# Attention rows and gate logits taken straight from the attention weights times [V, V's logits], in a fused attention and mixture-of-experts kernel

## Chip, cores and metric

One core of one Trainium2 chip runs the kernel. The metric is the device time of one execution in microseconds; a comparison takes the median of several executions. Engines are called by the names of the profile: PE (TensorE, its matrix instructions), PEld (TensorE's weight loads), DVE (VectorE), ACT (ScalarE), POOL (GpSimd), SP (SyncE, which here only issues DMAs).

## The reference, cut to what matters

Three parts follow each other. The change lies in the first; the other two are most of the time.

```python
# attention: 8 batches, 8 heads, 576 positions, 64 wide; K and V are averaged over groups of 8 positions
k_p = k.reshape(B, H, 72, 8, D).mean(axis=3)
v_p = v.reshape(B, H, 72, 8, D).mean(axis=3)
scores = np.matmul(q, k_p.transpose(0, 1, 3, 2)) / np.sqrt(D)
attn = np.exp(scores - scores.max(-1, keepdims=True))
attn = attn / (attn.sum(-1, keepdims=True) + 1e-09)
x = np.matmul(attn, v_p)                     # -> x: 4608 tokens x 512
# mixture of experts: 8 experts, 512 -> 1024 -> 512, the best two for each token
noisy = x @ w_gate + np.log1p(np.exp(x @ w_noise)) * noise
top2, weights = best_two(noisy)              # softmax over the two
x = sum(weights * (np.maximum(x @ w1[e], 0) @ w2[e]) for the two e)
# last layer: 512 -> 2048 -> 512
h = x @ w_in
out = (h - np.tanh(h)) @ w_out
```

## The kernel before, in words

The attention part is one loop over 36 tiles of 128 tokens (`NT` = 36). A tile holds 128 tokens of all 8 heads; four of the 36 tiles lie across the end of a batch and have rows of two batches ("mixed" tiles). A batch is four tiles, or five, counted from its first one: the first tiles of the eight batches, called T0, are 0, 4, 9, 13, 18, 22, 27 and 31. The loop is software-pipelined by hand: iteration t works on several tiles, each at another step. Every engine executes its own instructions in the order in which the program wrote them, so a wait of one instruction holds up all that stand behind it on that engine.

An iteration t of the loop does, in this order:

- `st_exps(t)`: ACT, eight exponentials, one per head, with sums.
- `st_xT(t-4)`: ACT copies the transposed x of an earlier tile from PSUM.
- first halves of the steps listed in `pe_step` for this t (PE: `vt`, `vs`, `kb`).
- `st_norm(t-1)` and `st_g(t-6)`: DVE. `st_norm` makes the reciprocals of the sums (`sm`, `rc`), `st_g` scales the rows of a finished tile (`xr`), scales its logits (`lg`) and adds them over the heads (`lz`); `xr` goes to DRAM by a DMA of SP.
- `st_attT(t-2)`: PE, five transposes of the weights into two PSUM tiles, and two ACT copies out of them.
- `st_q(t+2)`: PE transposes of q, and an ACT copy.
- `st_scores(t+1)`: PE; DVE takes two row maxima (`mx`), one for each half of the heads.
- `st_x(t-5)`: PE multiplies the transposed x by `wgn`, which is [identity, gate weights, noise weights]: it turns x back into rows and makes the logits beside them, in the tile `px`.
- second halves of the `pe_step` jobs, and then the jobs listed in `at_step` for this t (DVE and POOL work on K and V of coming batches, and weights of the next part).
- `st_av(t-3)`: PE, V times transposed weights, which gives x transposed.

Between them `tick` writes a few rows of the gate's work at a time (`gate_jobs`: top two, positions, lists of tokens per expert), for the tiles already finished, mostly on DVE.

Per batch, K and V (a `kt` or `vt` tile of 2560 elements per partition for each) are reduced over the 8 positions in three additions of 1280, 640 and 320 elements. The first was POOL's, the others DVE's. For K a `ke` product and the `kb` transposes follow; for V a maximum `vm`, its transpose (`vt`), its power of two (`vs`), and the product `vb` with a per-row scale `of8`, which writes `VB`.

PSUM has four buffers of the tag `pt` (transposes, small products, transposed x), two of `psc` (scores) and one of `px`. The instruction that first writes a buffer waits until the last reader of its former content is done.

The loop runs 42 iterations (36 and 6 more, in which the pipeline empties). The gate's last group of tiles and the gathering of the first rows for the experts happen in those last ones; then the experts' matmuls start (the line that writes `ph` from `x0T` and `pair`).

Of the kernel before, what the change touches and what calls it, by code (L numbers as in the profile page):

```python
# [10 lines left out]
F32 = mybir.dt.float32  # L11
# [4 lines left out]
OP = mybir.AluOpType  # L16
# [921 lines left out]
def attention(nc, tc, st, V):  # L938
# [52 lines left out]
    def warm(n, tag="px"):  # L991

        if tag == "px":
            p = ps.tile([128, HP, 256], F32, name="px", bufs=1)[:, 0:2].rearrange("p a c -> p (a c)")
        else:
            p = ps.tile([128, 4 * SP], F32, name=tag, bufs=2)
        for _ in range(n):
            nc.tensor.matmul(p, calm[:, 0:128], calm[:, 0:p.shape[1]], start=True, stop=True)
# [24 lines left out]
    ts(before, rowi, 0.0, None, op0=OP.is_gt)  # L1023
    ones = ep.tile([128, 128], BF16, name="ones")
    nc.vector.memset(ones, 1.0)
    wgn = one.tile([128, HP, 128 + 4 * E], F32, name="wgn")
    nc.vector.memset(wgn[:, :, 128:], 0.0)
    nc.vector.tensor_copy(wgn[:, :, 0:128], identf[:, None, :].to_broadcast([128, HP, 128]))
    nc.vector.memset(idx, 0)
    slot = ep.tile([128, 128], F16, name="slot")  # L1030
    nc.gpsimd.iota(slot, pattern=[[1, 128]], base=0, channel_multiplier=0, allow_small_or_imprecise_dtypes=True)
# [6 lines left out]
    for i in range(2):
        for w, o in ((w_gate, 0), (w_noise, E)):
            o += 128 + 2 * E * i  # L1040
            nc.sync.dma_start(wgn[64 * i:64 * i + 64, :, o:o + E], w.rearrange("(m i p) e -> i p m e", i=2, p=64)[i])
# [12 lines left out]
    def prep_jobs(b, first=False):  # L1054
        tl = {}

        def kpool():
            add(nc.vector, b, "k", 2)
            add(nc.vector, b, "k", 1)
            tl["ke"] = wk.tile([128, 5, 2, D], F32, name="ke", bufs=1)  # L1060
            tt(tl["ke"], KV[b, "k"][:, :, 0:1].to_broadcast([128, 5, 2, D]), odd[:, :, :, None].to_broadcast([128, 5, 2, D]),
               op=OP.mult)

        def vpool():
            add(nc.vector, b, "v", 2)
            add(nc.vector, b, "v", 1)
            tl["va"] = KV[b, "v"]

        def vmax():
            tl["vm"] = wk.tile([128, 1], F32, name="vm")  # L1070
            nc.vector.tensor_reduce(tl["vm"], tl["va"][:, :, 0], axis=AX.XY, op=OP.max, apply_absolute_value=True)

        def vmaxT():
            p = ps.tile([1, 128], F32, name="pt", bufs=4)
            nc.tensor.transpose(p, tl["vm"], identf)
            yield
            tl["vx"] = wk.tile([1, 1], F32, name="vx")
            nc.vector.tensor_reduce(tl["vx"], p, axis=AX.X, op=OP.max)

        def vscale():  # L1080
            p = ps.tile([128, 1], F32, name="pt", bufs=4)
            nc.tensor.matmul(p, ones1, tl["vx"], start=True, stop=True)
            yield
            m = wk.tile([128, 3], F32, name="vs")
            pow2(nc, m, p)
            of8 = wk.tile([128, 5, 4], F32, name="of8")
            ts(of8, of, m[:, 2:3], None, op0=OP.mult)
            tt(VB[b % 2].rearrange("p c (j d) -> p c j d", d=D), tl["va"][:, :, 0:1].to_broadcast([128, 5, 4, D]),
               of8[:, :, :, None].to_broadcast([128, 5, 4, D]), op=OP.mult)
            lo, hi = b * S, b * S + S  # L1090
            t0, t1 = lo // 128, -(-hi // 128)
            for t in range(t0, t1):
                o0, o1 = max(lo - 128 * t, 0), min(hi - 128 * t, 128)
                if o1 - o0 < 128:
                    ts(isc[o0:o1, t:t + 1], m[o0:o1, 1:2], 1.0 / 128, None, op0=OP.mult)
            f0, f1 = -(-lo // 128), hi // 128
            ts(isc[:, f0:f1], m[:, 1:2].to_broadcast([128, f1 - f0]), 1.0 / 128, None, op0=OP.mult)

        def kbd():
            for i, (c0, c1) in enumerate(((0, 3), (3, 5))):  # L1100
                w = cuts[c1] - cuts[c1 - 1]
                p = ps.tile([128, 4, 128], F32, name="pt", bufs=4)[:, 0:c1 - c0, 0:w]
                for c in range(c0, c1):
                    nc.tensor.transpose(p[:, c - c0], tl["ke"][:w, c].rearrange("p i d -> p (i d)"), identf[:w, :w])
                o = KB[b % 2][:, cuts[c0]:cuts[c1]].rearrange("p (c n) -> p c n", n=w)
                nc.scalar.activation(o, p, AF.Copy, scale=1.0 / 512)
            yield
        return dict(k=kpool, v=vpool, vm=vmax, vt=vmaxT, vs=vscale, kb=kbd)

    QT, SC, AT, ATT, PV, XT, SM, RC = {}, {}, {}, {}, {}, {}, {}, {}  # L1110

# [47 lines left out]
            nc.scalar.activation(a[:w, c0:c1], p, AF.Copy)  # L1159
        ATT[t] = a  # L1160

    def st_av(t):
        a = ATT.pop(t)
        p = ps.tile([128, HP, 128], F32, name="pt", bufs=4)
        for o, n, b, s in runs(t):
            for m in range(HP):
                cs = [c for c in range(5) if cuts[c] < 2 * SP * (m + 1) and 2 * SP * m < cuts[c + 1]]
                for c in cs:
                    w, j = cuts[c + 1] - cuts[c], 128 * (m + 1 - c)
                    nc.tensor.matmul(p[:, m, o:o + n], VB[b % 2][:w, c, j:j + 128], a[:w, c, o:o + n],  # L1170
                                     start=(c == cs[0]), stop=(c == cs[-1]))
        PV[t] = p

    def st_xT(t):
        XT[t] = wk.tile([128, HP, 128], F32, name="xT")
        nc.scalar.activation(XT[t], PV.pop(t), AF.Copy)

    def st_x(t):

        xT = XT.pop(t)  # L1180
        p = PX[t] = ps.tile([128, HP, 256], F32, name="px", bufs=1)
        for m in range(HP):
            nc.tensor.matmul(p[:, m, 0:128 + 4 * E], xT[:, m], wgn[:, m], start=True, stop=True)

    PX = {}
# [12 lines left out]
    def psum(shape):
        return ps.tile(shape, F32, name="pt", bufs=4)
# [72 lines left out]
    def lists(t0, n, row, col):  # L1272
# [4 lines left out]
        for c0 in range(0, n, LT):  # L1277
# [72 lines left out]
    at(0, P[0]["v"])  # L1350
    at(0, P[0]["vm"])
    at_pe(1, P[0]["vt"])
    at_pe(2, P[0]["vs"])
    TB = {b: (b * S) // 128 for b in range(B)}
    for b in range(1, B):
        P[b] = prep_jobs(b)
        T0 = TB[b]
        d = 1 if b == 1 else 0
        if b > 1:
            at(T0 - 8, load_kv, b, "k")  # L1360
            at(T0 - 7, load_kv, b, "v")
        at(max(T0 - 5, 0), add, nc.gpsimd, b, "k", 4)
        at(max(T0 - 4, 1), P[b]["k"])
        at(max(T0 - 4, 1), add, nc.gpsimd, b, "v", 4)
        at(max(T0 - 3, 2), P[b]["v"])
        at_pe(T0 - (1 if b == 1 else 2), P[b]["kb"])
        at(T0 - 1 + d, P[b]["vm"])
        at_pe(T0 + d, P[b]["vt"])
        at_pe(T0 + 1 + d, P[b]["vs"])
    at(2, lambda: nc.sync.dma_start(nz, noise.rearrange("(t p) e -> p t e", p=128)))  # L1370

    def early_x():
# [37 lines left out]
            at(36 + j, c2.high, j, nc.scalar)  # L1410
            at(37 + j, c2.low, j)
    ex = []
    for t in range(NT + 6):
        now[0] = t
        if t + 4 < NT:
            load_q(t + 4)
        if t < NT:
            st_exps(t)
        if 0 <= t - 4 < NT:
            st_xT(t - 4)  # L1420
        pj = [f() for f in pe_step.get(t, [])]
        for g in pj:
            next(g)
# [7 lines left out]
        if 0 <= t - 6 < NT:
            st_g(t - 6)
            if t - 6 in groups:
                pend.append(gate_jobs(*groups[t - 6]))
        tick()
        if 0 <= t - 2 < NT:
            st_attT(t - 2)
# [73 lines left out]
```

## Time and profile before

| | |
|---|---|
| time, median of 3 runs (lowest to highest) | 1882.54 us (1879.2 to 1884.77) |
| profiled execution, its own time | 1878.27 us |
| its span | 1876.5 us |
| mean granted clock of TensorE over the span | 0.989 |
| busy in the span: PE, DVE, ACT, POOL | 1801.6, 1201.6, 787.6, 246.2 us |
| start of the experts' first matmul | 279.21 us |

The span is the part of the execution that the profile shows; a count of the stages is made on it. The busy sums are of the whole span, of which the loop of the change is only the first 279 us.

### The profile page before, as it was taken

What the parts mean: (1) busy time and instruction counts of PE and PEld (TensorE: products, weight loads), DVE (VectorE), ACT (ScalarE), POOL (GpSimd) and SP (SyncE); (2) the same over time, 40 slices, a digit from 0 to 9 for tenths busy, and PEclk for the clock granted to TensorE, in tenths of its full rate; (3) what the DMA queues carried; (4) which work ended last, traced back from release to release, by engine and by line L of the source; (5) the groups of instructions that cost most, each with busy time, mean ns of one, the idle gap of its engine ahead of it and who ended that gap; (6) DMA issues with size and microseconds to landing.
All of it is one profiled execution on the core that took longest, in us unless ns stands there. A gap on an engine that the chain in (4) does not pass through costs nothing. (4 is left out here: it accounts for less than half of the span.)

```text
span 1876.5 us, 25894 instructions
## 1 busy us (share of the span) xinstructions
PE 1801.6 (96%) x9639; PEld 965.3 (51%) x9640; DVE 1201.6 (64%) x2454; ACT 787.6 (42%) x1875; POOL 246.2 (13%) x220
## 2 busy tenths in 40 slices
PE   7987989999999999999999999999999999999998
PEld 4886974445445454545454444444444444444443
DVE  5779886666576565665665557566566657566654
ACT  5675741433434342434334245343434434343432
POOL 3112011312103030100101202010010101010000
PEclk8998999999999999999999999999999999999999
DMA  9656423464554645554544422221111213120100
GB/s 229 182 144 188 111 75 101 127 152 129 143 158 124 162 123 144 135 148 131 144 124 100 128 67 75 59 65 45 46 51 40 58 34 84 40 57 29 23 23 24
DMA packets 225616, 188.57 MB, mean 100 GB/s; under 512 B 161920, under 2 KB 170112, under 8 KB 225472
## 3 DMA queue, kind: packets, MB, share of 16 engines
q1 hardware_dynamic: 213312, 147.48, 28.6%
q0 software_dynamic: 11904, 38.81, 8.1%
q8 instruction: 79, 1.29, 0.3%
q14 instruction: 65, 0.53, 0.1%
q10 hardware_dynamic: 256, 0.46, 0.1%
HBM read 117.62 MB, written 41.55 MB: 85 GB/s over the span
## 5 line engine op out<-in xcount | busy, mean ns | idle before, releaser
L345 ACT ACTIVATE hT<-ph 128x512 f16<-128x512 f32 (+2 forms) x192 | 96.8, 505 | 453.9 <-PE ph L343 450.8
L341 PE MATMUL ph<-xTp,pair 128*128 128x384 f16 (+2 forms) x736 | 245.3, 333 | 12.4 <-DMA xTp<-xp 4.8
L342 PE MATMUL ph<-xTp,pair 128*128 128x384 f16 (+2 forms) x736 | 244.9, 333 | 0.4 <-DVE xTp L322 0.4
L343 PE MATMUL ph<-xTp,pair 128*128 128x384 f16 (+2 forms) x736 | 244.9, 333 | 0.0
L863 DVE SCALAR_TENSOR_TENSOR t<-ph,cinf,hs 128x512 f32<-128x512 f32 x141 | 105.7, 749 | 202.3 <-ACT hs L862 202.2
L346 DVE SCALAR_TENSOR_TENSOR hT<-ph,hT 128x512 f16<-128x512 f32 (+2 forms) x192 | 110.7, 577 | 186.8 <-ACT hT L345 186.6
L862 ACT ACTIVATE hs<-ph,cinf 128x512 f32<-128x512 f32 x141 | 96.5, 684 | 301.4 <-PE ph L755 301.4
L907 PE MATMUL py<-wo,gT 128*128 128x512 f16 x576 | 218.3, 379 | 0.8 <-DVE gT L856 0.8
L365 PE MATMUL py<-pair,hT 128*128 128x512 f16 x576 | 218.3, 379 | 0.3 <-DVE hT L346 0.3
L363 PE MATMUL py<-pair,hT 128*128 128x512 f16 x576 | 218.3, 379 | 0.0
L364 PE MATMUL py<-pair,hT 128*128 128x512 f16 x576 | 218.3, 379 | 0.0
L905 PE MATMUL py<-wo,gT 128*128 128x512 f16 x576 | 218.3, 379 | 0.0
L906 PE MATMUL py<-wo,gT 128*128 128x512 f16 x576 | 218.3, 379 | 0.0
L753 PE MATMUL ph<-yT,wi 128*128 128x512 f16 x512 | 194.0, 379 | 0.0
L754 PE MATMUL ph<-yT,wi 128*128 128x512 f16 x512 | 194.0, 379 | 0.0
L755 PE MATMUL ph<-yT,wi 128*128 128x512 f16 x512 | 194.0, 379 | 0.0
L301 POOL DMA_INDIRECT xg<-x_d,idx x75 | 79.6, 1061 | 627.5 <-DVE xp L328 486.0
L695 POOL DMA_INDIRECT y<-y_d,ridx x64 | 60.7, 949 | 577.5 <-DVE y L706 355.1
L341 PEld LDWEIGHTS <-pair 128*128 128x128 f16 x768 | 75.2, 98 | 84.7 <-issue 24.6
L342 PEld LDWEIGHTS <-pair 128*128 128x128 f16 x768 | 75.3, 98 | 60.2 <-issue 4.5
L343 PEld LDWEIGHTS <-pair 128*128 128x128 f16 x768 | 75.2, 98 | 57.4 <-issue 1.2
L866 ACT ACTIVATE qa<-th,bias 128x512 f32<-128x512 f32 x144 | 102.4, 711 | 1.4 <-DVE th L864 1.4
(270 smaller groups left out, 3014.6 us busy)
## 6 DMA issues: line engine op xcount, KB each, us to landing
stage<-in_moe_w SPq DMA_DIRECT2D x64, 512.0 KB, 6.6
y_d<-ys SPq DMA_DIRECT2D x82, 256.0 KB, 2.1
x_d<-xr SPq DMA_DIRECT2D x36, 256.0 KB, 2.3
out<-o SPq DMA_DIRECT2D x36, 256.0 KB, 2.1
qt<-in_q SPq DMA_DIRECT2D x32, 256.0 KB, 6.5
raw<-in_moe_w_in SPq DMA_DIRECT2D x32, 256.0 KB, 3.4
raw<-in_moe_w_out SPq DMA_DIRECT2D x32, 256.0 KB, 2.8
kt<-in_k SPq DMA_DIRECT2D x7, 768.0 KB, 6.2
```

The source lines that it names most:

```text
L341: nc.tensor.matmul(p[:, :nt], w[:, 0, m, s], x[:, 0, m, :nt], start=(m == 0), stop=False)
L342: nc.tensor.matmul(p[:, :nt], w[:, 0, m, s], x[:, 1, m, :nt], start=False, stop=False)
L343: nc.tensor.matmul(p[:, :nt], w[:, 1, m, s], x[:, 0, m, :nt], start=False, stop=(m == KD - 1))
L363: nc.tensor.matmul(p, h[:, 0, s], w[:, 0, f], start=(f == 0), stop=False)
L364: nc.tensor.matmul(p, h[:, 0, s], w[:, 1, f], start=False, stop=False)
L365: nc.tensor.matmul(p, h[:, 1, s], w[:, 0, f], start=False, stop=(f == KF - 1))
L753: nc.tensor.matmul(p, wi[:, 0, m, s], y[:, 0, m], start=(m == 0), stop=False)
L754: nc.tensor.matmul(p, wi[:, 0, m, s], y[:, 1, m], start=False, stop=False)
L755: nc.tensor.matmul(p, wi[:, 1, m, s], y[:, 0, m], start=False, stop=(m == self.KD - 1))
L905: nc.tensor.matmul(p, g[:, 0, s], wo[:, 0, f], start=(f == 0), stop=False)
L906: nc.tensor.matmul(p, g[:, 0, s], wo[:, 1, f], start=False, stop=False)
L907: nc.tensor.matmul(p, g[:, 1, s], wo[:, 0, f], start=False, stop=(f == KF - 1))
```

## The change

The product of weights and V is turned round. Before, V was the stationary operand and the transposed weights moved, which gave x transposed; x then had to be copied and multiplied by the identity to become rows. Now the transposed weights are stationary and V moves, which gives rows at once, straight into `px`. For the logits, each head's V in `VB` has 16 further columns (`DG` = 80 instead of 64): V times the gate and noise weights of that head. They are made once per batch by two new steps, `vlog1` (five PE transposes of the pooled V into two `pt` buffers, ACT copies) and `vlog2` (five matmuls into two `pt` buffers, five DVE products into `VB`). `st_xT` and `st_x` are gone, so `st_g` works on tile t-4 instead of t-6 and the loop ends after 40 iterations. The first addition of K and of V and one product of the gate's lists (`l_col`) go from POOL to DVE. `wgn` is replaced by `wgh`, which holds the two weights only and takes two DMAs instead of four.

```diff
@@ vlog1, vlog2: new
+        def vlog1():
+            tl["vT"] = wk.tile([D, H * SP], F32, name="vT", bufs=1)
+            pp = []
+            for c0, c1 in ((0, 3), (3, 5)):
+                w = cuts[c1] - cuts[c1 - 1]
+                p = ps.tile([128, 4, 128], F32, name="pt", bufs=4)[:D, 0:c1 - c0, 0:w]
+                for c in range(c0, c1):
+                    nc.tensor.transpose(p[:, c - c0], tl["va"][:w, c, 0], identf[:w, :w])
+                pp.append((p, tl["vT"][:, cuts[c0]:cuts[c1]].rearrange("p (c n) -> p c n", n=w)))
+            yield
+            for p, o in pp:
+                nc.scalar.activation(o, p, AF.Copy)
+
+        def vlog2():
+            pp = []
+            for c0, c1 in ((0, 3), (3, 5)):
+                w = cuts[c1] - cuts[c1 - 1]
+                p = ps.tile([128, 4 * H * 2 * E], F32, name="pt", bufs=4)
+                for c in range(c0, c1):
+                    o = (c - c0) * H * 2 * E
+                    nc.tensor.matmul(p[:w, o:o + H * 2 * E], tl["vT"][:, cuts[c]:cuts[c + 1]], wgh.rearrange("p h e -> p (h e)"),
+                                     start=True, stop=True)
+                pp.append(p)
+            yield
+            G = 2 * E
+            for c, j0, j1 in ((0, 2, 4), (1, 0, 4), (2, 0, 4), (3, 0, 4), (4, 0, 2)):
...
+                tt(VB[b % 2][:w, c, j0:j1, D:], pp[c // 3][:w, o:o + (j1 - j0) * G].rearrange("p (j e) -> p j e", e=G),
+                   tl["of8"][:w, c, j0:j1, None].to_broadcast([w, j1 - j0, G]), op=OP.mult)
@@ st_av, st_xT, st_x
+    AV = ((1, 0, 4, 0), (0, 2, 4, 0), (2, 1, 2, 0), (3, 0, 4, 1), (2, 2, 4, 1), (4, 0, 2, 1))
     def st_av(t):
-        p = ps.tile([128, HP, 128], F32, name="pt", bufs=4)
+        p = PX[t] = ps.tile([128, 2, 512], F32, name="px", bufs=1)
         for o, n, b, s in runs(t):
-            for m in range(HP):
...
-                    nc.tensor.matmul(p[:, m, o:o + n], VB[b % 2][:w, c, j:j + 128], a[:w, c, o:o + n],
-                                     start=(c == cs[0]), stop=(c == cs[-1]))
+            for i, (c, j0, j1, k) in enumerate(AV):
+                w, h = cuts[c + 1] - cuts[c], 2 * (c - 1) + j0 - 4 * k
+                nc.tensor.matmul(p[o:o + n, k, DG * h:DG * (h + j1 - j0)], a[:w, c, o:o + n],
+                                 VB[b % 2][:w, c, j0:j1].rearrange("p j d -> p (j d)"), start=(i % 3 == 0), stop=(i % 3 == 2))
-    def st_xT(t):
...
-    def st_x(t):
...
@@ gate_jobs
-            nc.gpsimd.tensor_tensor(C[:, :, :, 1], C0, head[:, t0 + c0:t0 + c0 + m, None, None].to_broadcast([128, m, 2, K]),
+            tt(C[:, :, :, 1], C0, head[:, t0 + c0:t0 + c0 + m, None, None].to_broadcast([128, m, 2, K]),
@@ the times of the batch's jobs (d is 1 for the second batch, else 0)
-        at(max(T0 - 5, 0), add, nc.gpsimd, b, "k", 4)
-        at(max(T0 - 4, 1), P[b]["k"])
-        at(max(T0 - 4, 1), add, nc.gpsimd, b, "v", 4)
-        at(max(T0 - 3, 2), P[b]["v"])
+        at(max(T0 - 4, 0), add, nc.vector, b, "k", 4)
+        at(max(T0 - 3, 1), P[b]["k"])
+        at(max(T0 - 2, 1), add, nc.vector, b, "v", 4)
+        at(max(T0 - 1, 2), P[b]["v"])
         at_pe(T0 - (1 if b == 1 else 2), P[b]["kb"])
         at(T0 - 1 + d, P[b]["vm"])
         at_pe(T0 + d, P[b]["vt"])
+        at_pe(T0 + d, P[b]["g1"])
         at_pe(T0 + 1 + d, P[b]["vs"])
+        at_pe(T0 + 1 + d, P[b]["g2"])
@@ the loop
-    for t in range(NT + 6):
+    for t in range(NT + 4):
```

Three places show how the instructions now stand. The first is PE in iteration 9, where batch 2 begins (T0 = 9). In the kernel before, the transpose of `vm` is followed by the transposes of the weights (`at`, into two `pt` buffers), of q (`qt`), and the scores.

```order
L1075 MATMUL pt_864<-identf_64,vm_837 1x128 [waits DVE_49,Activation_49]
L1158 MATMUL pt_876<-identf_64,at_699 128x128 [waits Activation_49]
L1158 MATMUL pt_876<-identf_64,at_699 128x128 x2
L1158 MATMUL pt_881<-identf_64,at_699 96x128 x2
L1116 MATMUL pt_885<-identf_64,qt_697 128x128 [waits DMAHW4_49,Activation_49]
L1116 MATMUL pt_885<-identf_64,qt_697 128x128 x3
L1126 MATMUL psc_892<-kb0_152,qT_818 128x144 x2
```

The changed kernel has the same place so; `vt0` is the pooled V of batch 2.

```order
L1072 MATMUL pt_869<-identf_64,vm_847 1x128 [waits DVE_49,Activation_49]
L1103 MATMUL pt_872<-identf_64,vt0_110 64x128 [waits DMAHW3_49,Activation_49]
L1103 MATMUL pt_872<-identf_64,vt0_110 64x128 x2
L1103 MATMUL pt_876<-identf_64,vt0_110 64x96 [waits Activation_49]
L1103 MATMUL pt_876<-identf_64,vt0_110 64x96
L1187 MATMUL pt_889<-identf_64,at_724 128x128 x3
L1187 MATMUL pt_894<-identf_64,at_724 96x128 [waits Activation_49]
L1187 MATMUL pt_894<-identf_64,at_724 96x128
L1145 MATMUL pt_898<-identf_64,qt_722 128x128 [waits DMAHW4_49,Activation_49]
L1145 MATMUL pt_898<-identf_64,qt_722 128x128 x3
L1155 MATMUL psc_905<-kb0_152,qT_831 128x144 x2
```

Two `pt` tiles came in ahead of the weights' transposes. They and the tile of `vm` are read only in the second half of the iteration, so three of the four `pt` buffers are taken, and the second transpose tile (96x128) has a wait for ACT that it did not have. Iteration 10, with the matmuls of `vlog2`, has the same shape.

The second place is DVE in iteration 10, from the row maxima on. Before, it held the scale of batch 2's V and the additions of V of batch 3:

```order
L1129 TENSOR_REDUCE mx<-psc 128x4 x2
L100 TENSOR_SCALAR vs<-pt 128x1
L101 TENSOR_SCALAR vs<-vs 128x1
L102 TENSOR_SCALAR vs<-vs 128x1
L1087 TENSOR_SCALAR of_984<-of,vs 128x20
L1088 TENSOR_TENSOR vb_154<-vt_110,of_984 128x1280
L1095 TENSOR_SCALAR isc<-vs 64x1
L1097 TENSOR_SCALAR isc<-vs 128x4
L969 TENSOR_TENSOR vt_111<-vt_111 128x5x128
L969 TENSOR_TENSOR vt_111<-vt_111 128x5x64
```

Now it holds the scale of batch 2's V, the five products of `vlog2`, and the additions and the `ke` product of K of batch 3:

```order
L1158 TENSOR_REDUCE mx<-psc 128x4 x2
L100 TENSOR_SCALAR vs<-pt 128x1
L101 TENSOR_SCALAR vs<-vs 128x1
L102 TENSOR_SCALAR vs<-vs 128x1
L1084 TENSOR_SCALAR of_988<-of,vs 128x20
L1085 TENSOR_TENSOR vb_154<-vt_110,of_988 128x20x64
L1092 TENSOR_SCALAR isc<-vs 64x1
L1094 TENSOR_SCALAR isc<-vs 128x4
L1125 TENSOR_TENSOR vb_154<-pt,of_988 128x2x16
L1125 TENSOR_TENSOR vb_154<-pt,of_988 128x4x16 x2
L1125 TENSOR_TENSOR vb_154<-pt,of_988 96x4x16
L1125 TENSOR_TENSOR vb_154<-pt,of_988 96x2x16
L970 TENSOR_TENSOR kt_109<-kt_109 128x5x128
L970 TENSOR_TENSOR kt_109<-kt_109 128x5x64
L1058 TENSOR_TENSOR ke<-kt_109,odd 128x640
```

K's work moved one iteration later, behind the scale of the batch before; `ke` is now the last DVE row ahead of iteration 11.

The third place is PE at the head of iteration 11, where batch 3's K is transposed (`kb`). Before:

```order
L1104 MATMUL pt_1016<-identf_64,ke_911 128x128 [waits Activation_49]
L1104 MATMUL pt_1016<-identf_64,ke_911 128x128 x2
L1104 MATMUL pt_1021<-identf_64,ke_911 128x96 [waits Activation_49]
L1104 MATMUL pt_1021<-identf_64,ke_911 128x96
L1158 MATMUL pt_1035<-identf_64,at_852 128x128 [waits DVE_49]
```

Now its first row names DVE among what it waits for:

```order
L1133 MATMUL pt_1023<-identf_64,ke_1000 128x128 [waits DVE_49,Activation_49]
```

The transposes of K kept their place, and what makes their operand moved to one iteration ahead of it.

## Rows read from the trace of the kernel before

**Rows 1.** Windows between starts of `sm` in iterations 5, 9, 13, 31, 36, then the rest.

```profile
core 0: us, PE busy (x) PEld busy (x) DVE busy (x) ACT busy (x) POOL busy (x), PEclk, DMA share, GB/s
46.69:74.39 27.70, 24.01 (x168) 23.06 (x169) 21.44 (x45) 15.23 (x70) 6.08 (x2) 0.88 0.77 201
74.39:96.47 22.08, 21.99 (x186) 20.70 (x185) 17.78 (x48) 17.37 (x78) 2.89 (x1) 1.00 0.59 174
96.47:224.30 127.83, 106.38 (x864) 101.07 (x863) 107.06 (x275) 87.55 (x390) 23.50 (x9) 0.93 0.56 152
224.30:251.96 27.66, 26.41 (x225) 25.16 (x224) 21.17 (x67) 20.54 (x92) 3.04 (x2) 1.00 0.13 49
251.96:279.20 27.24, 20.85 (x180) 19.27 (x180) 22.58 (x70) 9.88 (x20) 5.54 (x5) 1.00 0.30 92
320.00:1876.00 1556.00, 1530.90 (x7651) 735.62 (x7648) 955.49 (x1790) 602.61 (x1098) 183.12 (x175) 1.00 0.34 91
```

**Rows 2.** Timeline of all engines: iterations 9 and 10, parts.

```profile
start us, us, engine line op out<-in xcount [idle before <-releaser]
79.25 1.33 DVE L969 TENSOR_TENSOR kt<-kt 128x640 f32<-128x640 f32 x2
...
80.61 0.82 DVE L1061 TENSOR_TENSOR ke<-kt,odd 128x640 f32<-128x640 f32 x1
...
81.36 0.16 DVE L1144 TENSOR_SCALAR sm<-sm 128x8 f32<-128x8 f32 x1
...
81.75 0.52 PEld L1158 LDWEIGHTS pt<-identf,at 128*128 128x128 f32 x5
...
82.26 0.46 PEld L1116 LDWEIGHTS pt<-identf,qt 128*128 128x128 f32 x4
...
82.39 0.76 ACT L1159 ACTIVATE aT<-pt 128x384 f32<-128x384 f32 x2 [0.19 <-PE pt L1158]
82.56 0.37 DVE L1196 TENSOR_REDUCE lz<-lg 128x16 f32<-128x128 f32 x1
82.68 1.04 PEld L1126 LDWEIGHTS psc<-kb,qT 128*128 128x128 f32 x8
...
83.05 0.60 ACT L1118 ACTIVATE qT<-pt 128x512 f32<-128x512 f32 x1
83.48 0.95 DVE L1129 TENSOR_REDUCE mx<-psc 128x4 f32<-128x288 f32 x2 [0.55 <-PE psc L1126]
83.65 1.13 PEld L1183 LDWEIGHTS px<-wgn,xT 128*128 128x128 f32 x8
...
83.98 0.32 ACT L1140 ACTIVATE at<-psc,mx 128x72 f32<-128x72 f32 x1 [0.33 <-DVE mx L1129]
...
84.35 0.15 DVE L100 TENSOR_SCALAR vs<-pt 128x1 f32<-128x1 f32 x1
...
84.72 1.89 PEld L1170 LDWEIGHTS pt<-aT,vb 128*128 128x128 f32 x16
...
85.18 1.49 DVE L1088 TENSOR_TENSOR vb<-vt,of 128x1280 f32<-128x1280 f32 x1
...
86.27 0.24 ACT L1140 ACTIVATION_READ_ACCUMULATOR at<-psc,mx 128x1 f32 x1
```

**Rows 3.** Timeline of all engines: POOL's addition beside DVE, and PE after it.

```profile
175.56 2.87 POOL L969 TENSOR_TENSOR kt<-kt 128x1280 f32<-128x1280 f32 x1
175.67 4.11 DVE L1088 TENSOR_TENSOR vb<-vt,of 128x1280 f32<-128x1280 f32 x1
...
182.17 0.42 DVE L1289 TENSOR_TENSOR l_row<-slot,g_row 128x256 f16<-128x256 f16 x1
...
184.31 2.10 PEld L1183 LDWEIGHTS px<-wgn,xT 128*128 128x128 f32 x8 [9.37 <-issue]
```

**Rows 4.** Groups by form of PE, DVE and POOL, 38 to 280 us.

```profile
L1183 PE MATMUL px<-wgn,xT 128*128 128x160 f32 x288 | 50.1, 321 | 20.6 <-DVE lg L1195 20.5 <-ACT xT L1176 0.2
...
L1289 DVE TENSOR_TENSOR l_row<-slot,g_row 128x256 f16<-128x256 f16 x26 | 16.4, 647 | 0.0
...
L1144 DVE TENSOR_SCALAR sm<-sm 128x8 f32<-128x8 f32 x33 | 12.2, 370 | 0.0
...
L969 POOL TENSOR_TENSOR vt<-vt 128x1280 f32<-128x1280 f32 x6 | 17.5, 2919 | 37.2 <-DVE mx L1129 14.3 <-DMA vt<-in_v 13.8 <-DVE g_p L1227 5.0
```

More of the change, by code (lines that the diff above doesn't have):

```diff
@@ L952, in attention @@
     KV = {}
+    DG = D + 2 * E
     cuts = (0, 128, 256, 384, 480, 576)
@@ L993, in warm @@
         if tag == "px":
-            p = ps.tile([128, HP, 256], F32, name="px", bufs=1)[:, 0:2].rearrange("p a c -> p (a c)")
+            p = ps.tile([128, 2, 512], F32, name="px", bufs=1)[:, 0]
         else:
@@ L1009, in attention @@
     KB = [one.tile([128, 2 * HP * SP], F32, name=f"kb{i}") for i in range(2)]
-    VB = [one.tile([128, 5, 4 * D], F32, name=f"vb{i}") for i in range(2)]
+    VB = [one.tile([128, 5, 4, DG], F32, name=f"vb{i}") for i in range(2)]
     of = one.tile([128, 5, 4], F32, name="of")
@@ L1025, in attention @@
     nc.vector.memset(ones, 1.0)
-    wgn = one.tile([128, HP, 128 + 4 * E], F32, name="wgn")
-    nc.vector.memset(wgn[:, :, 128:], 0.0)
-    nc.vector.tensor_copy(wgn[:, :, 0:128], identf[:, None, :].to_broadcast([128, HP, 128]))
+    wgh = one.tile([D, H, 2 * E], F32, name="wgh")
     nc.vector.memset(idx, 0)
@@ L1037, in attention @@
     load_q(3)
[L1038 to L1041, printed above, removed]
+    for w, o in ((w_gate, 0), (w_noise, E)):
+        nc.sync.dma_start(wgh[:, :, o:o + E], w.rearrange("(h p) e -> p h e", p=D))
     load_kv(1, "v")
@@ L1085, in vscale @@
             pow2(nc, m, p)
-            of8 = wk.tile([128, 5, 4], F32, name="of8")
+            of8 = tl["of8"] = wk.tile([128, 5, 4], F32, name="of8")
             ts(of8, of, m[:, 2:3], None, op0=OP.mult)
-            tt(VB[b % 2].rearrange("p c (j d) -> p c j d", d=D), tl["va"][:, :, 0:1].to_broadcast([128, 5, 4, D]),
+            tt(VB[b % 2][:, :, :, 0:D], tl["va"][:, :, 0:1].to_broadcast([128, 5, 4, D]),
                of8[:, :, :, None].to_broadcast([128, 5, 4, D]), op=OP.mult)
@@ L1097, in vscale @@
             ts(isc[:, f0:f1], m[:, 1:2].to_broadcast([128, f1 - f0]), 1.0 / 128, None, op0=OP.mult)
+        def vlog1():
[23 more added lines that the diff above has]
+            for c, j0, j1 in ((0, 2, 4), (1, 0, 4), (2, 0, 4), (3, 0, 4), (4, 0, 2)):
+                w = cuts[c + 1] - cuts[c]
+                o = (c % 3) * H * G + (2 * (c - 1) + j0) * G
+                tt(VB[b % 2][:w, c, j0:j1, D:], pp[c // 3][:w, o:o + (j1 - j0) * G].rearrange("p (j e) -> p j e", e=G),
+                   tl["of8"][:w, c, j0:j1, None].to_broadcast([w, j1 - j0, G]), op=OP.mult)
         def kbd():
@@ L1107, in kbd @@
             yield
-        return dict(k=kpool, v=vpool, vm=vmax, vt=vmaxT, vs=vscale, kb=kbd)
+        return dict(k=kpool, v=vpool, vm=vmax, vt=vmaxT, vs=vscale, kb=kbd, g1=vlog1, g2=vlog2)
     QT, SC, AT, ATT, PV, XT, SM, RC = {}, {}, {}, {}, {}, {}, {}, {}
@@ L1160, in st_attT @@
         ATT[t] = a
+    PX = {}
+    AV = ((1, 0, 4, 0), (0, 2, 4, 0), (2, 1, 2, 0), (3, 0, 4, 1), (2, 2, 4, 1), (4, 0, 2, 1))
     def st_av(t):
         a = ATT.pop(t)
-        p = ps.tile([128, HP, 128], F32, name="pt", bufs=4)
+        p = PX[t] = ps.tile([128, 2, 512], F32, name="px", bufs=1)
         for o, n, b, s in runs(t):
-            for m in range(HP):
-                cs = [c for c in range(5) if cuts[c] < 2 * SP * (m + 1) and 2 * SP * m < cuts[c + 1]]
-                for c in cs:
-                    w, j = cuts[c + 1] - cuts[c], 128 * (m + 1 - c)
-                    nc.tensor.matmul(p[:, m, o:o + n], VB[b % 2][:w, c, j:j + 128], a[:w, c, o:o + n],
-                                     start=(c == cs[0]), stop=(c == cs[-1]))
@@ L1172, in st_av @@
-        PV[t] = p
-    def st_xT(t):
-        XT[t] = wk.tile([128, HP, 128], F32, name="xT")
-        nc.scalar.activation(XT[t], PV.pop(t), AF.Copy)
-    def st_x(t):
[L1180 to L1185, printed above, removed]
+            for i, (c, j0, j1, k) in enumerate(AV):
+                w, h = cuts[c + 1] - cuts[c], 2 * (c - 1) + j0 - 4 * k
+                nc.tensor.matmul(p[o:o + n, k, DG * h:DG * (h + j1 - j0)], a[:w, c, o:o + n],
+                                 VB[b % 2][:w, c, j0:j1].rearrange("p j d -> p (j d)"), start=(i % 3 == 0), stop=(i % 3 == 2))
@@ L1187, in st_g @@
     def st_g(t):
-        p, rc = PX.pop(t), RC.pop(t)
+        p, rc = PX.pop(t)[:, :, 0:4 * DG].rearrange("p a (h c) -> p a h c", c=DG), RC.pop(t)
+        r = rc.rearrange("p (a h) -> p a h", a=2)[:, :, :, None]
         xr = wk.tile([128, DM], F32, name="xr", bufs=3)
-        r = rc.rearrange("p (m i) -> p m i", i=2)[:, :, :, None]
-        h = lambda a, n: a.rearrange("p m (i n) -> p m i n", n=n)
-        tt(xr.rearrange("p (m i n) -> p m i n", m=HP, i=2), h(p[:, :, 0:128], D), r.to_broadcast([128, HP, 2, D]), op=OP.mult)
+        tt(xr.rearrange("p (a h d) -> p a h d", a=2, d=D), p[:, :, :, 0:D], r.to_broadcast([128, 2, 4, D]), op=OP.mult)
@@ L1193, in st_g @@
         nc.sync.dma_start(x_d[128 * t:128 * t + 128, :], xr)
-        lg = wk.tile([128, HP, 2, 2 * E], F32, name="lg", bufs=1)
-        tt(lg, h(p[:, :, 128:128 + 4 * E], 2 * E), r.to_broadcast([128, HP, 2, 2 * E]), op=OP.mult)
-        nc.vector.tensor_reduce(lz[:, t], lg.rearrange("p m i e -> p e (m i)"), axis=AX.X, op=OP.add)
+        lg = wk.tile([128, 2, 4, 2 * E], F32, name="lg", bufs=1)
+        tt(lg, p[:, :, :, D:], r.to_broadcast([128, 2, 4, 2 * E]), op=OP.mult)
+        nc.vector.tensor_reduce(lz[:, t], lg.rearrange("p a h e -> p e (a h)"), axis=AX.X, op=OP.add)
@@ L1338, in at_pe @@
         pe_step.setdefault(t, []).append(f)
-        assert len(pe_step[t]) < 3
+        assert len(pe_step[t]) < 4
     P = {0: prep_jobs(0)}
@@ L1352, in attention @@
     at_pe(1, P[0]["vt"])
+    at_pe(1, P[0]["g1"])
     at_pe(2, P[0]["vs"])
+    at_pe(2, P[0]["g2"])
     TB = {b: (b * S) // 128 for b in range(B)}
@@ L1418, in attention @@
             st_exps(t)
-        if 0 <= t - 4 < NT:
-            st_xT(t - 4)
         pj = [f() for f in pe_step.get(t, [])]
@@ L1430, in attention @@
             st_norm(t - 1)
[L1431 to L1434, printed above, removed]
+        if 0 <= t - 4 < NT:
+            st_g(t - 4)
+            if t - 4 in groups:
+                pend.append(gate_jobs(*groups[t - 4]))
         tick()
@@ L1445, in attention @@
             st_scores(t + 1)
-        if 0 <= t - 5 < NT:
-            st_x(t - 5)
         tick()
```

## The prediction

> **What bounds the kernel now.** I first read the busy time by stage. After 320 us PE is busy 1530.90 of 1556.00 us, so that stage is PE's and the change doesn't touch it. Before that no engine is full: from iteration 13 to 31 PE is busy 106.38 and DVE 107.06 of 127.83 us, at a mean clock of 0.93 [rows 1]. Only iterations 9 to 12 are full: PE 21.99 of 22.08 us at clock 1.00. So the loop is bound by PE where nothing disturbs it, and by waits elsewhere.
>
> Then I read one undisturbed iteration in the timeline. PE loads for the weights' transposes (0.52), q (0.46), scores (1.04), x (1.13) and V times weights (1.89): 5.0 of some 5.3 us. ACT's exponentials run from 83.98 to 86.51. DVE needs 1.57 from `sm` to the end of `lz` and 0.95 for `mx`, and has room [rows 2].
>
> Last I read the waits. PE's longest kind is `px` on DVE's `lg`, 20.6 us in the loop [rows 4]. DVE itself is held by POOL: `vb` took 4.11 beside POOL's addition where it takes 1.49 alone, and PE stood 9.37 us after it [rows 2, 3]. `sm` has a mean of 0.370 over 33 where one alone takes 0.16, `l_row` 0.647 over 26 where one alone takes 0.42 [rows 2 to 4]. That is 33 × 0.21 + 26 × 0.23 + 2.6 = 15.5 us of DVE held by POOL, the few other rows of that kind left out.
>
> **What goes, what comes.** Per tile the x matmuls go (1.13 of PE) and ACT's copy of transposed x (as long as `qT`, 0.60). V times weights was 16 records; it is now twelve, of 1200 columns twice over. The eight x records have 160 columns each, so 1.13/1280 us per column: 2.12 us, against 1.89 [rows 2]. An undisturbed iteration of PE would be 0.52 + 0.46 + 1.04 + 2.12 = 4.1 to 4.2 us. (A mixed tile has everything twice in both kernels.)
>
> DVE gets the first additions, 1280 elements; `vb` has 1280 too: 1.49 each, 12 of them in iterations 5 to 35, 17.9 us [rows 2]. `l_col` has 800 elements: 0.93 by the same row, four or five times. The five products of `vlog2` are in no trace. From below, one is a `vs` row, 0.15; from above, half a `mx` pair, 0.48 [rows 2]; they have 32 or 64 elements from PSUM, nearer the small row, so 0.2 each, 1.0 a batch (0.75 to 2.4). `vlog1` is five transposes (0.52) and two ACT copies (0.76); `vlog2` ten records at 1.89/16, 1.2 us [rows 2]. Two DMAs fewer at the start are hidden by SP's other loads; the stores of `xr` come two iterations earlier on SP and nothing waits for them in the loop.
>
> **The order costs more than the rows.** Three new waits stand in PE's order. I follow batch 2's four iterations, with 0 at the first exponential of iteration 9, by start-to-start times of rows 2: transposes to ACT's copy 0.64; copies 0.45 and 0.31; q to its copy 0.79; scores to `mx` 0.80; `mx` to exponentials 0.50; exponentials 2.53.
>
> First, iteration 9. The V additions (1.33) and `vm` now stand right behind `mx`, so `vm` ends near 2.5, and `vlog1`'s transposes at 3.2. The weights' transposes have one PSUM buffer of four left: the first tile is copied from 4.0 to 4.45, the second by 5.3, and q only then takes the buffer. Scores start at 5.85, `mx` at 6.65; q's copy and `vlog1`'s two copies hold the exponentials to 7.45. `mx` to `mx`: 7.15 us.
>
> Second, iteration 10. V times weights to 9.0, `vlog2` to 10.5, then the same chain through one buffer: scores at 12.95, `mx` at 13.75. 7.1 us.
>
> Third, iteration 11. Behind that `mx` (to 14.7) DVE has the scale of V (`vs` to the end of `vb`, 84.35 to 86.67, and two small rows: 2.6), `vlog2`'s products 1.0, K's additions 1.33 and `ke` 0.82 [rows 2]: 5.75, so `ke` ends at 20.5. PE is through at 16.1 and `kb` waits for `ke`: 4.4 us idle. Before, `ke` stood an iteration earlier and was long done. Behind the waiting `kb` on PE are the weights' transposes, q and the scores, for which DVE waits at its next `mx`, and ACT behind that. So `kb` (five transposes, 0.5), weights, q, scores to `mx`: 2.5 us, and `mx` at 22.95 follows.
>
> After the 9.37 us wait the px loads took 2.10 for 1.13, half the clock [rows 2, 3]: at half the clock some 1.8 us of work in them take twice as long, `mx` at 24.75. If the clock held, seven batches would be 1.8 x 7 = 13 us shorter in all: 1885. By the Trainium skill's page "TensorE: Matmul & The Clock Gate", Part 1, an idle array falls to half its clock and activity releases it; the trace agrees (1.13 against 2.10), and by it this change, which makes new idle time, would pay on PE itself for what waits on DVE; by the rule the sum stays at its 1898.
>
> Iteration 12 goes at PE's pace, 4.2 us. So iteration 13's `mx` is at 28.95; iteration 9's was at -0.5, and the four take 29.4 against 22.08 [rows 1]: +7.3. A batch of five has the K addition with the scale of V (5.7) and `ke` an iteration later; the single `px` buffer then waits for `lg` behind them, and `kb` waits about 1.4: I get 31.5.
>
> **The sum over the loop.** Up to iteration 4: +0.5 (`vlog1` and `vlog2` of batch 0, 1.7 us of PE, partly in the place of the warm-up matmuls). Iterations 5 to 8: 29.4 and some 2.4 of weight rows against 27.70: +4. Iterations 9 to 12: +7.3. Iterations 13 to 30 are batches of 5, 4, 5, 4: 121.8 against 127.83, if gate and weight rows all fall into gaps. These: 107.06 less 4 × 17.78 (a batch without them, rows 1) less two iterations of 2.5 is 31, less 18/31 of the 15.5 held some 22, and with `l_col` and two iterations' earlier start 27. If all of them lengthen the loop, +21; if none, -6. DVE is the late one in half of the iterations, so I take half, 13: +7. Iterations 31 to 35: two batch iterations of 7.1, three of 4.2 and half of 6 us of gate rows: 30.0 against 27.66, +2.4. The tail was six iterations in 27.24 us; four at the same pace are 18, but DVE has 22.58 busy there that go on [rows 1]: 20, so -7. What doesn't fit lands in the experts' first group, where it delays PE by 0 to 3.5, taken 1.5.
>
> 0.5 + 4 + 7.3 + 7 + 2.4 - 7 + 1.5 = 15.7 us slower. The profiled execution had 1878.27 us (a span of 1876.5, 1.8 around it), 4.3 under the median 1882.54; I add to the median: 1898.
>
> **The rivals.** (a) Faster: DVE is the only bound and the new PE waits are hidden under its work. DVE's rows of iterations 5 to 35 were 21.44 + 17.78 + 107.06 + 21.17 = 167.45 [rows 1]; less 15.5 held, plus 17.9, 3.7 and 7.0, are 180.6; with the 0.55 idle ahead of `mx` [rows 2] in 31 iterations, 197.6 against 205.27. With tail and ends -12.7: 1870. For it: the held rows are real, and x's matmul is gone. Against: in the order, PE's scores stand behind `kb` and the buffers, and DVE's next `mx` behind these. It decides if `kb` finds `ke` done, or the gaps stay under 2 us.
>
> (b) Gate rows all fall into the waits: +7 becomes -6, total +2.7: 1885. For it: they are short and written between the others. Against: they too stand in DVE's order, ahead of `mx` or `ke`.
>
> (c) The clock falls at most of the bank waits too: nine more at 1.8, +16: 1914. For it: PEclk was 0.88 and 0.93 in the stretches with waits [rows 1]. Against: the waits at the buffers are of one or two microseconds each.
>
> That the change doesn't do what it says I exclude: in the new order no tensor row of the loop is left on POOL.
>
> **How the numbers follow.** The forecast, slower by 8 to 24 us, has 0.54; (a) 0.16; (b) 0.16; (c) 0.14. 0.3% is 5.6 us, about what a measurement here can tell. Faster: (a) and a little of (b), 0.18. Same: the middle of (b) and (a)'s near end, 0.16. Slower: 0.66. The range leaves out the better half of (a) and the worse half of (c): 1872 to 1916; the likeliest case's own is 1890 to 1906.
>
> **What would show it.** In the profile after: `kb`'s transposes in the list of waits released by DVE's `ke`, 3 to 5 us in the short batches, with half-clock rows behind; the second transpose tile and q released by ACT's `aT`; no `sm`, `l_row` or `vb` beyond its own length; a tail of 20 us. A `kb` without wait, or 4.2 us iterations through iterations 9 to 12, would make the prediction wrong, and then (a) is right.

## The result, and the profile after

The changed kernel takes 1900.53 us (median of 4 runs, 1899.72 to 1902.11); the kernel before, run beside it, 1880.87. The ratio is 1.011, with a 95% interval of 1.0091 to 1.0128: slower by 1.1%, as forecast. The profiled execution has a span of 1897.9 us, 21.4 more than before.

First the windows of the changed kernel, between the same points as in [rows 1]: the starts of `sm` of iterations 5, 9, 13, 31 and 36, and the experts' first matmul.

```profile
core 0: us, PE busy (x) PEld busy (x) DVE busy (x) ACT busy (x) POOL busy (x), PEclk, DMA share, GB/s
48.43:77.86 29.43, 23.97 (x141) 19.92 (x141) 21.78 (x55) 15.79 (x78) 0.00 (x0) 0.88 0.74 205
77.86:108.05 30.19, 23.64 (x149) 20.01 (x149) 19.51 (x55) 16.16 (x72) 0.00 (x0) 0.89 0.55 149
108.05:251.80 143.75, 111.72 (x697) 92.79 (x697) 111.40 (x314) 82.83 (x383) 0.00 (x0) 0.89 0.49 130
251.80:284.19 32.39, 27.20 (x176) 21.97 (x177) 20.44 (x74) 17.70 (x84) 2.06 (x2) 0.95 0.18 57
284.19:303.35 19.16, 13.53 (x96) 10.90 (x96) 17.06 (x49) 6.83 (x12) 1.89 (x2) 0.96 0.21 70
```

Iterations 9 to 12, which PE had filled, are now 30.19 us with PE busy for 23.64 and DVE for 19.51: neither engine is full, so somebody waits for somebody. PEclk, 1.00 there before, is 0.89.

Who waits, in the view of the waits of the changed kernel, 38 to 300 us (in all, times, longest):

```profile
engine line waited for: us in total, times, longest us
...
DVE mx L1158 <- PE psc L1155: 48.6, 31, 3.9
...
PE pt L1133 <- DVE ke L1058: 11.4, 4, 4.7
PE pt L1187 <- ACT aT L1188: 9.3, 14, 1.0
...
PE pt L1145 <- ACT aT L1188: 7.4, 15, 0.9
...
PE pt L1133 <- DVE sm L1173: 3.6, 1, 3.6
...
PE pt L1133 <- DVE g_e L1283: 3.5, 1, 3.5
```

L1133 is `kb`: it waits six times, 18.5 us, and each time it starts as `ke` ends (in two of the six the view names the row that follows `ke` on DVE). L1187 is the second transpose tile, 14 times, and L1145 is q, 15 times: two iterations of each of seven batches.

The timeline of the changed kernel in iterations 10 and 11 shows both (start, length, engine; in brackets the idle time ahead):

```profile
86.02 0.31 PEld L1187 LDWEIGHTS pt<-identf,at 128*128 128x128 f32 x3
...
86.67 0.49 ACT L1188 ACTIVATE aT<-pt 128x384 f32<-128x384 f32 x1 [1.60 <-PE pt L1187]
...
87.21 0.17 PEld L1187 LDWEIGHTS pt<-identf,at 128*96 128x96 f32 x2 [0.88 <-ACT aT L1188]
...
87.67 0.38 ACT L1188 ACTIVATE aT<-pt 96x256 f32<-96x256 f32 x1 [0.51 <-PE pt L1187]
...
88.10 0.42 PEld L1145 LDWEIGHTS pt<-identf,qt 128*128 128x128 f32 x4 [0.72 <-ACT aT L1188]
...
89.29 0.95 DVE L1158 TENSOR_REDUCE mx<-psc 128x4 f32<-128x288 f32 x2 [3.36 <-PE psc L1155]
...
94.48 0.82 DVE L1058 TENSOR_TENSOR ke<-kt,odd 128x640 f32<-128x640 f32 x1
...
95.42 0.93 PEld L1133 LDWEIGHTS pt<-identf,ke 128*128 128x128 f32 x5 [3.80 <-issue]
...
97.29 0.87 PEld L1145 LDWEIGHTS pt<-identf,qt 128*128 128x128 f32 x4
...
98.14 1.99 PEld L1155 LDWEIGHTS psc<-kb,qT 128*128 128x128 f32 x8
```

From 86.0 to 88.1 PE and ACT take turns on one buffer: transposes, copy, transposes, copy, q. DVE has meanwhile waited 3.36 us for the scores. Then its rows run without a break to the end of `ke` at 95.3, PE stands 3.80 us ahead of `kb`, and behind it q takes 0.87 (0.42 the iteration before) and the scores 1.99, against 1.04 in [rows 2].

What the change was to take away is gone. In the groups by form of the changed kernel (38 to 280 us), `vb`, `sm` and `l_row` have their undisturbed lengths, where `sm` had a mean of 0.370 and `l_row` of 0.647 in [rows 4]:

```profile
L1085 DVE TENSOR_TENSOR vb<-vt,of 128x1280 f32<-128x1280 f32 x7 | 10.4, 1491 | 0.2
...
L1306 DVE TENSOR_TENSOR l_row<-slot,g_row 128x256 f16<-128x256 f16 x20 | 8.0, 409 | 0.0
...
L1173 DVE TENSOR_SCALAR sm<-sm 128x8 f32<-128x8 f32 x33 | 5.2, 159 | 0.0
```

### The profile page after: what moved, and what is told of

The parts are those of the page before. It is cut to its first block, busy times and chain, and to the rows that moved or that the text cites. A ratio compares the mean times of both kernels' runs of the same rounds, so it can differ in the third digit from the quotient of the medians.

```text
span 1897.9 us, 25191 instructions
## 1 busy us (share of the span) xinstructions
PE 1805.8 (95%) x9304; PEld 944.2 (50%) x9304; DVE 1207.2 (64%) x2514; ACT 776.4 (41%) x1855; POOL 192.9 (10%) x198
```

## The experiments

Theory A is that of the prediction: the change is slow by its order, `kb` behind a late `ke` and transposes behind taken buffers. Rival B: it is slow by volume, the additions that DVE now does, wherever they stand. Ratios are to the kernel before, run beside each. A difference in us between two changed kernels is one of medians from different sessions; the kernel before had medians of 1878.61 to 1882.83 us in them, so such a difference is good to some 4 us. The start of the experts' first matmul in the profiles (303.35 us in the changed kernel) is given beside the larger ones: it shows the loop alone.

**K earlier.** Edit of the changed kernel:

```diff
-        at(max(T0 - 4, 0), add, nc.vector, b, "k", 4)
-        at(max(T0 - 3, 1), P[b]["k"])
+        at(max(T0 - 5, 0), add, nc.vector, b, "k", 4)
+        at(max(T0 - 4, 1), P[b]["k"])
```

> The changed kernel with K's first addition and K's pooling one iteration earlier (the iterations that they had before the change), all still on DVE; nothing else. Theory A (the order costs: kb waits for a ke that stands too near): the kb waits of 18.5 us in six batches and the half-clock rows behind them go, some 1.8 us five times, less what the same DVE rows delay an iteration earlier; 1874 to 1886 us against 1900.5. Rival B (the volume costs: 18 us of additions on DVE lengthen the loop wherever they stand): DVE does the same rows, so 1897 to 1903.

1888.18 us, ratio 1.003 (1.0014 to 1.0046): 12 us less, a little short of A's range, and outside B's. The experts start at 292.15, 11.2 earlier. The waits of `kb` for `ke` are gone from the view; DVE's waits for the scores fell from 48.6 to 39.0 us. The rest of the loss lies elsewhere.

**vlog's PE work behind the scores.** The transposes of `vlog1` and the matmuls of `vlog2` go to the second half of their iterations, `vlog1`'s copies to the head of the next:

```diff
 def vlog1():
+    yield
     tl["vT"] = wk.tile([D, H * SP], F32, name="vT", bufs=1)
...
         pp.append((p, tl["vT"][:, cuts[c0]:cuts[c1]].rearrange("p (c n) -> p c n", n=w)))
-    yield
-    for p, o in pp:
-        nc.scalar.activation(o, p, AF.Copy)
+    tl["pp"] = pp
 def vlog2():
+    for p, o in tl["pp"]:
+        nc.scalar.activation(o, p, AF.Copy)
+    yield
     pp = []
...
         pp.append(p)
-    yield
```

> The changed kernel with vlog1's transposes and vlog2's matmuls written behind the scores in their iterations, and vlog1's two ACT copies at the head of the next one, so that the transposes of the weights and q find more than one pt buffer. Theory A (buffers and order): the waits of the second transpose tile (9.3 us) and of q (8.7 us) shrink to half or less, DVE's mx comes earlier in two iterations of each batch; 1884 to 1896 us. Rival B (DVE volume): no row of DVE goes, 1897 to 1903.

1866.45 us, ratio 0.9912 (0.9889 to 0.9934). That is 34 us less, over twice what I expected; the experts start at 270.14, 33.2 earlier. No DVE row was taken away, so B falls. The waits of this kernel:

```profile
ACT kb L1136 <- PE pt L1134: 18.9, 6, 4.9
DVE mx L1159 <- PE psc L1156: 18.7, 22, 2.2
...
PE pt L1146 <- ACT aT L1189: 1.7, 4, 0.4
```

q waits 4 times instead of 15, and DVE's waits for the scores are down by 30 us, most of the gain. The entries for the buffers, 9.3 and 7.4 us, had understated their price. The timeline above suggests why: in the chain ACT's copies and PE's transposes are busy in turn, and only the pauses between them are booked as waits. A part of the gain may be the clock, which had fallen in some of these iterations too (see below).

**Both.**

> Both edits of the two runs before it together. Theory A: the two waits stand in different iterations, so the gains add up: 1862 to 1880 us, at or below the kernel before. Rival B: 1897 to 1903. If kb's wait and the buffers' waits hide each other, the gain is that of the larger alone.

1855.67 us, ratio 0.9854 (0.9831 to 0.9877): 45 us below the changed kernel, and the two gains (12 and 34) add up; the experts start at 259.79, 43.6 earlier. This version is faster than both kernels. Its windows from `sm` of iteration 5 on:

```profile
46.62:69.92 23.30, 22.27 (x157) 18.93 (x158) 21.21 (x54) 16.27 (x80) 0.00 (x0) 1.00 0.94 254
69.92:90.36 20.44, 19.52 (x140) 16.57 (x139) 17.94 (x54) 15.01 (x70) 0.00 (x0) 1.00 0.81 218
90.36:210.82 120.46, 102.55 (x696) 86.67 (x697) 111.02 (x314) 81.74 (x383) 0.00 (x0) 0.94 0.59 156
```

DVE is busy 111.02 of 120.46 us, with the same rows as in the changed kernel (111.40), in 23 us less. So in this stretch the volume probably sets the pace now; no run with fewer rows on DVE and nothing else changed tests it. In iterations 9 to 12 it is PE that is full, 19.52 of 20.44 us.

**V earlier too**, on top of both (V's additions at T0 - 3 and T0 - 2):

> e3_both with V's additions one iteration earlier too, so that vm no longer stands right ahead of its transpose. If e3_both's loop is bound by DVE's rows: no change, 1852 to 1859 us. If the wait for vm still counts: 1846 to 1852.

1855.5 us, ratio 0.9865 (0.9842 to 0.9888): no change, as expected if DVE's rows set the pace: the place of these rows no longer matters.

**Order or buffers?** The second experiment moved work on PE and freed buffers in one. To part them, I first only created the tiles early.

> e2_v_second, but the four pt buffers of vlog1 and vlog2 are taken at the places where the changed kernel takes them (ahead of the transposes of the weights and of q) and only written behind the scores. It tells the two halves of that edit apart. If held buffers are the cost: the waits of the second transpose tile and of q come back, 1890 to 1902 us. If it was the place of vlog's own matmuls ahead of the scores on PE (0.7 and 1.2 us a batch, and vm's wait ahead of all): 1864 to 1872, as e2_v_second.

1864.9 us, as the second experiment. It tells nothing: PE's instructions stood with the same waits as there, since a tile that nothing has written takes no buffer. The next run writes each of the four early (shown are the two of `vlog1`; those of `vlog2` are written in the same way):

```diff
+            for p in bufs:
+                nc.tensor.matmul(p[:, 0, 0:8], calm[:, 0:128], calm[:, 0:8], start=True, stop=True)
             yield
```

> e9_hold, whose buffers turned out not to be held (a tile that is not yet written takes no buffer): now each of the four is written ahead of the transposes of the weights and q by a matmul of 8 columns on zeros, so that it is truly taken there; vlog's own matmuls stay behind the scores. If held buffers are the cost: q and the second transpose tile wait for ACT again, 1888 to 1904 us. If the place of vlog's matmuls on PE was: 1864 to 1873, as e2_v_second and e9_hold.

1896.23 us, ratio 1.0099 (1.007 to 1.0128), 31 us more for four tiny matmuls a batch. Its waits have the old entries back:

```profile
DVE mx L1165 <- PE psc L1162: 43.8, 28, 4.1
...
PE pt L1194 <- ACT aT L1195: 9.8, 14, 1.4
...
PE pt L1152 <- ACT aT L1195: 6.5, 14, 0.5
```

The experts start at 299.94, against 268.23 in the run before. So held buffers are the cost; where vlog's own matmuls stand is worth some 4 us, the difference from the changed kernel, and about what such a difference can tell.

**The clock.** 18 matmuls on zeros fill the wait ahead of `kb` in the changed kernel:

```diff
+        if t in [TB[b] - 2 for b in range(2, B)]:
+            warm(18, "psc")
         for g in pj:
             next(g)
```

> The changed kernel with 18 warm-up matmuls (128x288 bf16, on zeros, read by nobody) written ahead of kb in the six iterations in which kb waits for ke; they end before ke does. Theory: the half clock behind the wait is part of the price, 1.8 us five or six times; the stretches behind kb run at full clock and the time is 1889 to 1896 us against 1900.5. Rival: behind kb another engine sets the pace and the clock is only seen, not paid: 1898 to 1903.

1897.26 us (1894.52 to 1902.14), ratio 1.0095 (1.0067 to 1.0122), an interval that overlaps that of the changed kernel (1.0091 to 1.0128). PE's weight loads behind `kb` in iteration 11 ran at full clock:

```profile
93.15 0.53 PEld L1133 LDWEIGHTS pt<-identf,ke 128*128 128x128 f32 x5 [1.39 <-DVE ke L1058]
...
94.28 0.42 PEld L1145 LDWEIGHTS pt<-identf,qt 128*128 128x128 f32 x4
94.67 1.04 PEld L1155 LDWEIGHTS psc<-kb,qT 128*128 128x128 f32 x8
```

0.53, 0.42 and 1.04 where the changed kernel has 0.93, 0.87 and 1.99: the half clock is real, and filling the gap removed it here. Its price is not resolved. The medians differ by 3.3 us and the spans of the two profiled executions by 5.2 (1897.9 and 1892.7), below the 9 to 11 that I had put on it. But in these two the experts start at 294.76 and 303.35: the loop is 8.6 us shorter, near my figure, and the stage behind it, which the edit doesn't touch, 3.4 longer. It is one execution of each, and that of the filled kernel is the fastest of its four.

The clock also falls where I had not counted it. In the changed kernel the scores' loads run wholly or mostly at half clock (1.74 to 1.99 us for 1.04) behind four of the six waits of `kb`, and in seven of the fourteen iterations with buffer waits. Iteration 13 is one of these:

```profile
110.38 0.17 PEld L1187 LDWEIGHTS pt<-identf,at 128*96 128x96 f32 x2 [1.24 <-ACT aT L1188]
111.28 0.72 PEld L1145 LDWEIGHTS pt<-identf,qt 128*128 128x128 f32 x4 [0.73 <-ACT aT L1188]
111.98 1.99 PEld L1155 LDWEIGHTS psc<-kb,qT 128*128 128x128 f32 x8
```

The filled kernel has fewer such places, and its granted clock from 40 to 284 us is 0.96 against 0.90.

**The additions.** Three runs place them. The kernel before with its additions and `l_col` on DVE, at POOL's old times (three lines call DVE instead of POOL):

> The kernel before with its 14 first additions and l_col on DVE at the times that POOL had; x still through transposed x and wgn. Theory A: DVE has room (40 us idle in iterations 5 to 35), and its rows held by POOL go: 1864 to 1882 us against 1880.9. Rival B (volume): 18 us of additions on DVE less some 10 of held rows, or all of them: 1888 to 1898.

1874.34 us, ratio 0.996 (0.9944 to 0.9975). The move off POOL is a small gain by itself.

The direct product with vlog's work behind the scores, and the additions and `l_col` on POOL at the old times:

> The direct product with vlog1 and vlog2 behind the scores (as in e2_v_second), and the additions and l_col on POOL at the times of the kernel before. If the direct product is a gain by itself once it doesn't take the buffers: 1858 to 1872 us, about e3_both plus the 8.5 that the additions on DVE gave the kernel before. If the gain of e3_both is that of the additions alone: 1875 to 1885.

1870.21 us, ratio 0.994 (0.9917 to 0.9962). So each half of the change gains alone, 0.4% and 0.6%, and both together, well placed, 1.5% (0.9854).

The changed kernel with the first additions on POOL, in the changed order:

> The changed kernel with the 14 first additions back on POOL, in the iterations in which the changed kernel has them on DVE; all else as in the changed kernel. Order theory: ke stays behind the scale of V and kb keeps waiting, the buffers too; DVE loses 20 us of rows but is held again by POOL: 1892 to 1908 us. Rival (the additions' volume on DVE costs): 1878 to 1888.

1912.03 us, ratio 1.0171 (1.0145 to 1.0197): 11.5 us more than the changed kernel, a little beyond the range of the order theory and far from the rival's. The timeline in iteration 10:

```profile
95.50 2.88 POOL L970 TENSOR_TENSOR kt<-kt 128x1280 f32<-128x1280 f32 x1 [24.19 <-DMA kt<-in_k]
...
95.81 3.77 DVE L970 TENSOR_TENSOR kt<-kt 128x640 f32<-128x640 f32 x2
...
99.61 0.82 DVE L1058 TENSOR_TENSOR ke<-kt,odd 128x640 f32<-128x640 f32 x1
```

POOL's addition is that of the next batch's K. It starts here when its load has landed, whatever DVE does, and it holds DVE's K additions (1.33 in [rows 2], 3.77 here) right ahead of `ke`, for which PE waits. Over the loop `kb` waits 23.3 us instead of 18.5. That is 4.8 of the 11.5 us; where the rest lies is not shown.

**The gate's rows.** The largest miss of the sum was in iterations 13 to 30 (below). In this run the gate's rows are written only from iteration 31 on, so its whole time (1920.39 us, one run) is no measure of them.

```diff
 def tick(n=1):
+    if 13 <= now[0] < 31:
+        return
+    n *= 5 if now[0] >= 31 and looping[0] else 1
```

> The changed kernel, in which no row of the gate is written in iterations 13 to 30; they all come later, in longer runs, so the whole time says nothing. What counts is the stretch from sm of iteration 13 to that of 31, 143.75 us in the changed kernel. If the gate's rows lengthened it, as the walk without them has it: 121 to 128 us (only weight rows are left). If it was too short for other reasons (mixed tiles, waits of PE that the walk lacks): 135 to 144.

The stretch, from `sm` of iteration 13 to that of 31:

```profile
107.70:234.68 126.98, 102.84 (x655) 85.58 (x655) 90.10 (x222) 79.01 (x375) 0.00 (x0) 0.93 0.54 148
```

126.98 us against 143.75: the gate's work lengthened the stretch by 16.8 us. On DVE that work was 21.3 us (111.40 less 90.10); the run also took 42 matmuls off PE and 8 instructions off ACT, so the 16.8 are not DVE's rows alone. The stretch without the gate is still 5.2 us longer than the 121.8 of the walk. It holds weight rows, some 10 us on DVE:

```profile
L158 DVE SCALAR_TENSOR_TENSOR pair<-stage,wsc,pair 128x1024 f16<-128x1024 f32 x4 | 5.1, 1272 | 0.0
L126 DVE TENSOR_REDUCE am<-stage 128x1 f32<-128x1024 f32 x4 | 4.8, 1210 | 0.0
```

## Why the prediction was right, point by point

**The whole.** 1898 was forecast and 1900.53 measured, 15.7 slower against 19.7. The mechanism is shown: freeing the buffers and moving `ke` takes back 45 us with the same rows on DVE. The volume on DVE, rival (a)'s only bound, cannot have set the pace before that. Rival (a) needed `kb` to find `ke` done; it didn't.

**The walk of iterations 9 to 12.** 29.4 us were worked out and 30.19 measured (+8.1 for +7.3). `kb` waited 3.8 us in iteration 11, where the walk had 4.4, the loads behind it ran at half clock, and the chain through one buffer looked as walked. From one `mx` to the next the four took 6.9, 7.4, 10.3 and 5.2 us, where the walk had 7.15, 7.1, 11.0 and 4.2; so the sum is closer than its last two parts, whose errors cancel. In the other batches `kb` waited 3.5 to 4.7 us behind a batch of four (the walk: 4.4), and 2.0 and 0.9 behind one of five (1.4). The parts: twelve weight loads for the direct product took 2.16 in the undisturbed case for 2.12; the five products of `vlog2` 0.67 for 1.0; `l_col` 0.99 for 0.93.

**The other terms.** From the windows: iterations 5 to 8 are +1.7 (forecast +4), up to iteration 5 the loop lost 1.7 (0.5), 31 to 35 are +4.7 (+2.4), and the tail is 19.16 against 27.24, -8.1 (-7).

**The mis-sized term** is that of iterations 13 to 30: the walk's 121.8 us, and half of 27 us of gate and weight rows, "I take half, 13: +7". The stretch took 143.75, so +15.9, and 22 more than the walk. The rows were more, some 31 us on DVE (21 of the gate, 10 of the weights). And of the gate's work 16.8 us lengthened the loop, four fifths of its 21.3 on DVE and not half. The other 5.2 us may be weight rows, or the half clock behind buffer waits, which the walk did not have; no run parts these. The profile gives only a part of the reason for the four fifths: some gate rows stand in iterations where DVE had no gap (15 to 17 and 24 to 26 have 0.10 to 0.17 us idle each). These six are together 3.3 us longer than in the run without gate rows; iterations 18, 21 and 23 are 10.0 longer, and why these three is not shown.

**What balanced it.** That the total came within 4 us (15.7 against 19.7) is partly luck: the 8.9 us too few in iterations 13 to 30 meet errors of the other sign. Iterations 5 to 8 lost 2.3 us less than forecast and the tail gained 1.1 more. From the experts' first matmul on, the changed kernel's profiled execution is 2.7 us shorter (1594.55 against 1597.29), where 1.5 longer was forecast. The change doesn't touch that stage, and over the profiles of all these runs it varies from 1593.7 to 1598.2, so the 2.7 are no more than its scatter. Had it been as forecast, the changed kernel would have been some 4 us slower.

**The clock.** The half clock was 1.8 us of each batch in the walk. That it stands behind the gaps is shown; its price is not (3.3 us at the median, 8.6 in the loop of one execution, against 9 to 11). Rival (c), a lower clock at most of the buffer waits too, came in part: in seven such iterations the scores ran at half clock, while two of the six waits of `kb` had none behind them. Its time, 1914, did not come; the forecast's seven places with half clock were eleven in the profile, and the time that this cost is inside the terms above.

**What I weighed too low.** The walk had the buffers' chain in it (7.15 and 7.1 us for two iterations of each batch), but the signs that it listed begin with `kb`. By the runs the buffers cost 34 us, `kb` 12.

## What to carry to other kernels

A step that fills PSUM tiles early and reads them late costs what the others must then do in turn: look at how many buffers are left between its write and its last read, and not at its own length. A wait's entry in the list can understate that (here 16.7 us were booked and 34 gained), since engines that pass one buffer to and fro look busy; the idle time of the engine at the end of the chain (here DVE ahead of `mx`) shows it. And where an operand's maker moves nearer to its reader in a program order, count the rows that stand between the two on the maker's engine.

## What the runs showed that I had not expected

Four matmuls of 8 columns per batch, on data that nobody reads, cost 31 us by taking buffers. Filling PE's gaps brought the clock back behind `kb` (0.87 to 0.42 us for the same four loads), and yet the medians differ by 3.3 us only, which is not clear of the noise. And the clock fell at half of the buffer waits too, each of them little more than a microsecond.
